# A list product moved behind the last values, and the first pieces of w_out loaded into lasting buffers

## The chip, the core and the metric

The kernel runs on one core of a Trainium2 chip. The metric is the time of one execution on the device, in microseconds (us). Engines are named as in the profile: PE (TensorE, matmuls), DVE (VectorE), ACT (ScalarE), POOL (GpSimd), SP (SyncE, which only issues transfers here).

## The reference

```python
def reference(q, k, v, w_gate, w1, w2, w_in, w_out, s, b):
    # attention: 4 batches, 8 heads, 576 queries, head size 64; keys and values pooled by 8 (72 keys)
    k_p, v_p = (z.reshape(4, 8, 72, 8, 64).mean(axis=3) for z in (k, v))
    x = softmax(q @ k_p.T / 8) @ v_p                      # 2304 tokens of 512 numbers
    # routing: 8 experts, top 1; a token is kept if fewer than 576 before it chose its expert
    e = argmax(x @ w_gate); gate = softmax(x @ w_gate)[e]
    x = gate * (relu(x @ w1[e]) @ w2[e]) if kept else 0   # w1: 512x1024, w2: 1024x512
    # last layers, all tokens
    g = s * relu(x @ w_in) ** 2 + b                       # w_in: 512x2048
    return g @ w_out                                      # w_out: 2048x512
```

## The kernel before

Every product of two full-precision operands is made of three matmuls: each operand is split in a high half (a cast by ACT) and a low half (operand less high half, by DVE or POOL), and high x high, high x low and low x high are added up. Such a group over the four parts of a 512-long sum is twelve matmuls.

**Attention and routing** (to about 150 us). The queries are worked off in tiles of up to 128 tokens, batch after batch (five tiles each, the last one of 64). Values (L273, L275) come out of the PE, DVE scales them (L286 to L294) and leaves them in `xr` and the gate's logits in `lg`. `route(b, t0, t1)` then finds each token's expert (`rmx`, `rd`, `rval`, `rvm`, `roh`: a one-hot row) and its rank in the expert's list by matmuls with a triangle (L368 to L376), called "the ranking" below. Batch 4 is ranked twice, for its first three tiles and for its last two. `tail` makes of the ranks the operands of a list product (`rslot`, `rkey`, `tok`, `ohq`, `rlo`, `ohp`); `tok` holds the token numbers, which GpSimd makes in each tail (L401). `add_lists` is the list product (L434) and adds to `u_lists` (L437). `picked` (L689) reads from the lists the rows of the next unit, and `gather` fetches those with three indirect DMAs on GpSimd's queue (L938). These are Python generators; `step()` advances the queues `todo` (routes) and `tails` in turn, a generator that yields True is blocked for now, `window()` holds one until PE has a place for its matmul, and the list `work` holds the first unit's transposes (`x_part`, L952) and its layer 1 (L961, blocks f of twelve matmuls), which are set between them. The order of instructions on each engine is the order in which this Python code issues them.

**Experts.** `block(u)` works off units of 288 tokens of one expert (150 to 298 us), `small` the short rests of 144. SP loads w1 (L914) and w2 (L920) of the next unit by numbers that DVE makes (`u_i`, L682). Beside this DVE, ACT and POOL turn w_in from 64-bit floats, read as pairs of int32, into 32-bit ones: `Weights64` does a piece of 128x512 in four steps (L868 to L877: shift, or, or, |hi| on ACT, product), with the splitting of the piece before in step 1. `last(s)` is the end of the small experts: layer 2 of the last of them, store of its result yo to yt, and the first blocks of the last layers.

**Last layers.** `pair()` treats the first two units of 256 tokens together: `first(u, ..)` is layer 1 (L1034, twelve matmuls per block f) with `square` (relu by ACT, square by DVE, L1412) and `parts` (gh by ACT, gl by POOL or DVE, L1427); `second(u, ..)` is layer 2 (L1432). Between their blocks `conv(n)` does n steps of the conversion of w_out: 16 pieces `wo`, the splitting of a piece being a cast by ACT (L1386) and a difference by DVE (L1387), and a running sum of the pieces `raw[3]` (L1392). `load_out` loads the pieces on SP's queue (L1458). Layer 2 of the two units begins with the blocks 0 to 6; layer 1 of unit 1 is cut there in two. After the pair come six units, one after the other (`unit`, 442 to 600 us), and an end (`half`).

## Time and profile before

| | us |
|---|---|
| median of 3 runs | 660.01 (657.16 to 661.97) |
| the profiled execution | 664.05 |
| its span from the first to the last instruction | 662.3 |

| stretch of the span (us) | what is in it | PE busy (us) | granted clock (1 is full) |
|---|---|---|---|
| 108 to 152 | end of the attention, layer 1 of the first unit | 31.17 of 44 | 0.88 |
| 152 to 298 | units of the experts | 138.08 of 146 | 0.99 |
| 298 to 325 | small experts | 22.63 of 27 | 0.81 |
| 325 to 364 | end of the small experts, start of the pair | 33.10 of 39 | 0.99 |
| 364 to 409 | pair, to its second half of layer 1 | 38.77 of 45 | 0.50 (first 6 us), 0.98 |
| 409 to 442 | pair, end | 32.44 of 33 | 0.55 (first 6 us), 1.00 |
| 442 to 600 | six units | 158.00 of 158 | 1.00 |

PE is busy for 592.1 us in all (89% of the span), DVE for 365.5, ACT for 253.6 and POOL for 265.8. Busy PE time counts a matmul at the clock that it was given, so time lost to the lower clock is in it.

### The profile page before, as it was taken

To read this page: it belongs to the slowest core of one execution; us is meant where nothing else is said; L and a number is where in the kernel's file an instruction comes from. 1 tells how busy PE (TensorE), PEld (TensorE's weight loads), DVE (VectorE), ACT (ScalarE), POOL (GpSimd) and SP (SyncE) were. 2 spreads that over 40 slices of the span, in tenths; PEclk is the share of its full clock that TensorE was granted. 3 is DMA by queue.
4 is the path that set the end of the run, shared out by engine and by line. 5 is a ranking of instruction groups with operands and counts; after the bars stand their busy time and mean duration, and the time that the engine had idled before them with its cause. 6 is when DMAs were issued, how large, how long until landed. Compare 5 with 4: busy or idle time off the path is not lost. (4 is left out here: it accounts for less than half of the span.)

```text
span 662.3 us, 11174 instructions
## 1 busy us (share of the span) xinstructions
PE 592.1 (89%) x4005; PEld 549.5 (83%) x4005; DVE 365.5 (55%) x889; ACT 253.6 (38%) x620; POOL 265.8 (40%) x384
## 2 busy tenths in 40 slices
PE   5787888769899979997897996999999999999884
PEld 5787777669899979996897976889899899898784
DVE  4688798867968956661639999603312021131140
ACT  1354555436456645442336524304125033042130
POOL 5658434715154716012214301305725145144281
PEclk8799899879999989996999898999999999999998
DMA  8989665645649894844548111017300101000000
GB/s 165 199 183 190 163 195 171 215 126 197 232 155 295 282 309 148 282 135 156 169 142 350 38 33 32 1 33 286 111 17 1 49 17 29 29 9 2 35 2 20
DMA packets 67951, 86.12 MB, mean 130 GB/s; under 512 B 24713, under 2 KB 40073, under 8 KB 67856
## 3 DMA queue, kind: packets, MB, share of 16 engines
q1 hardware_dynamic: 57696, 71.34, 35.9%
q10 hardware_dynamic: 7712, 6.84, 3.4%
q0 software_dynamic: 2448, 6.82, 3.1%
q8 instruction: 42, 0.69, 0.5%
q14 instruction: 53, 0.43, 0.2%
HBM read 68.09 MB, written 17.58 MB: 129 GB/s over the span
## 5 line engine op out<-in xcount | busy, mean ns | idle before, releaser
L1432 PE MATMUL bank<-wo,gh 128*128 128x512 f32 (+1 forms) x412 | 119.3, 374 | 1.2 <-ACT wo L1386 1.0
L1427 POOL TENSOR_TENSOR gl<-rt,gh 128x256 fp32r<-128x256 f32 (+1 forms) x96 | 72.6, 761 | 110.8 <-ACT gh L1426 64.7
L1432 PEld LDWEIGHTS bank<-wo,gh 128*128 128x128 f32 x412 | 74.9, 188 | 15.1 <-ACT wo L1386 1.4
L1432 PE MATMUL bank<-wo,gl 128*128 128x512 f32 (+1 forms) x206 | 76.8, 373 | 0.0
L930 POOL TENSOR_TENSOR w1l<-kraw,w1h 128x128 fp32r<-128x128 f32 x96 | 52.6, 582 | 50.7 <-ACT w1h L923 50.6
L1108 PE MATMUL bank<-hs,w2h 128*128 128x288 f32 (+1 forms) x308 | 68.5, 311 | 4.7 <-issue 4.3
L1439 DVE SCALAR_TENSOR_TENSOR raw<-bank,sb,c_u 128x512 f32<-128x512 f32 (+1 forms) x14 | 9.9, 710 | 85.5 <-PE bank L1432 85.5
L1108 PEld LDWEIGHTS bank<-hs,w2h 128*128 128x128 f32 x308 | 50.7, 192 | 5.6 <-issue 5.1
L1411 ACT ACTIVATE rt<-tq 128x256 f32<-128x256 f32 (+1 forms) x26 | 9.5, 367 | 113.5 <-PE tq L1034 91.3
L1108 PE MATMUL bank<-hs,w2l 128*128 128x288 f32 (+1 forms) x148 | 44.7, 302 | 0.0
L1432 PEld LDWEIGHTS bank<-wo,gl 128*128 128x128 f32 x206 | 38.8, 188 | 6.8
L1412 DVE SCALAR_TENSOR_TENSOR rt<-bank,rt 128x256 f32<-128x256 f32 (+1 forms) x53 | 21.2, 401 | 38.3 <-ACT rt L1411 37.9
L1426 ACT CAST gh<-rt 128x256 fp32r<-128x256 f32 (+1 forms) x96 | 36.6, 381 | 6.5 <-DVE rt L1412 6.5
L938 POOL DMA_INDIRECT xg<-xd,u_idx x23 | 25.4, 1104 | 30.0 <-DVE r L288 16.7
L1440 POOL DMA_INDIRECT out_dram<-raw,it x12 | 12.0, 1001 | 62.6 <-DVE raw L1439 62.1
L1411 ACT ACTIVATE rt<-bank 128x256 f32<-128x256 f32 (+1 forms) x60 | 22.3, 371 | 35.4 <-PE bank L1034 27.0
L228 PE MATMUL sc<-kbd,qT 128*128 128x144 f32 (+1 forms) x152 | 25.4, 316 | 5.6 <-DVE r L286 3.6
L1412 DVE SCALAR_TENSOR_TENSOR rt<-tq,rt 128x256 f32<-128x256 f32 (+1 forms) x24 | 9.6, 400 | 36.3 <-ACT rt L1411 36.3
L1108 PEld LDWEIGHTS bank<-hs,w2l 128*128 128x128 f32 x148 | 28.4, 192 | 0.0
L228 PEld LDWEIGHTS sc<-kbd,qT 128*128 128x128 f32 (+1 forms) x152 | 21.9, 201 | 7.7 <-issue 5.1
L934 DVE TENSOR_TENSOR w2l<-vraw,w2h 128x512 fp32r<-128x512 f32 x39 | 27.4, 702 | 1.2 <-ACT w2h L933 0.5
L961 PE MATMUL bank<-xs,w1h 128*128 128x288 f32 (+1 forms) x120 | 26.1, 303 | 2.1 <-DVE hs L964 2.1
(485 smaller groups left out, 1705.0 us busy)
## 6 DMA issues: line engine op xcount, KB each, us to landing
kraw<-in_moe_w_dram SPq DMA_DIRECT2D x14, 1024.0 KB
vraw<-in_moe_w_dram SPq DMA_DIRECT2D x14, 1024.0 KB
wo<-in_moe_w_out_dram SPq DMA_DIRECT2D x16, 512.0 KB
c_raw<-in_moe_w_in_dram ACTq DMA_DIRECT2D x13, 512.0 KB
kraw<-in_k_dram SPq DMA_DIRECT2D x8, 576.0 KB
out_dram<-c_u SPq DMA_DIRECT2D x1, 4608.0 KB
q<-in_q_dram SPq DMA_DIRECT2D x16, 256.0 KB
xd<-xr SPq DMA_DIRECT2D x16, 256.0 KB
```

The source lines that it names most:

```text
L228: nc.tensor.matmul(sc[:n, p // 2, p % 2 * 144:p % 2 * 144 + 144], lhsT=q[:, p, :n], rhs=kbd[b % 2][:, p], start=True, stop=True)
L930: eng.tensor_sub(self.w1l[:, i, z], self.w1(i)[:, z], self.w1h[:, i, z])
L934: eng.tensor_sub(self.w2l[i], self.w2r[:, i], self.w2h[i])
L938: self.nc.gpsimd.indirect_dma_start(out=dst, out_offset=None, in_=self.xd[:have], in_offset=bass.IndirectOffsetOnAxis(ap=idx[:n], axis=0), ...
L961: self.nc.tensor.matmul(p, lhsT=l[:, f, k], rhs=r[k], start=n == 0, stop=n == 3 * KD - 1)
L1108: nc.tensor.matmul(py[d][:, :v.n], lhsT=l[f][:, d * P:d * P + P], rhs=r[f], start=f == 0 and i == 0, stop=f == KF - 1 and i == 2)
L1411: nc.scalar.activation(r, p, AF.Relu)
L1412: nc.vector.scalar_tensor_tensor(out=p if inside else r, in0=p, scalar=0.0, in1=r, op0=ALU.max, op1=ALU.mult)
L1426: nc.scalar.copy(h[:, :n], r)
L1427: (nc.gpsimd if p is None else nc.vector).tensor_sub(l[:, :n], r, h[:, :n])
L1432: nc.tensor.matmul(p[:, c], lhsT=g[:, j * P:j * P + P], rhs=wo[f][:, z, c], start=f == 0 and i == 0, stop=f == KF2 - 1 and i == 2)
L1440: i = nc.gpsimd.indirect_dma_start(out=dst, out_offset=bass.IndirectOffsetOnAxis(ap=ids, axis=0), in_=o[:, c], in_offset=None, bounds_chec ...
```

## The change

1. The token numbers of all tiles are made once, at the start of the attention, in `toks`; a tail reads its part of it.
2. The tail of batch 3 (`b == B - 2`) waits until one ranking short of the last, so its list product stands behind the last tile's values. With it the pick of unit 1's rows (L689) and their gather move behind the last ranking. Two parts of layer 1 instead of one follow now on the first ranking of batch 4, not on the second.
3. In `last_layers` the first three pieces of w_out use the buffers `c_raw` of w_in's raw pieces, which now live in a pool `keep` that lasts; the buffers `c_f` and `c_u` of the conversion come from the long-lived pools, and gl and the other pieces from a pool `side`. Twelve steps of the conversion (`conv(4 * FIRST)`) stand ahead of the first block. For these three pieces |hi| is made by DVE, the cast of the splitting and the start of the sum by GpSimd; `onesf` is set behind two of those casts.
4. `last` stores yo on ACT's queue, not SP's, splits y at f 6 and 7 and not 4 and 5, and the raw piece 15 of w_in is loaded three steps earlier.

```diff
+        toks = one.tile([P, B, NB], F32, name="toks")
+        nc.gpsimd.iota(toks, pattern=[[S, B], [P, NB]], base=0, channel_multiplier=1, allow_small_or_imprecise_dtypes=True)
...
-            nc.gpsimd.iota(tok, pattern=[[P, w]], base=b * S + t0 * P, channel_multiplier=1, allow_small_or_imprecise_dtypes=True)
...
-            v.scalar_tensor_tensor(out=tok, in0=r, scalar=float(cap), in1=tok, op0=ALU.is_lt, op1=ALU.mult)
+            v.scalar_tensor_tensor(out=tok, in0=r, scalar=float(cap), in1=toks[:, b, t0:t1], op0=ALU.is_lt, op1=ALU.mult)
...
+            while b == B - 2 and now[0] < N - 1:
+                yield True
             yield from window()
             add_lists(b, at_pe[0])
...
-                    for _ in range(2 if ranks == 1 else 1):
+                    for _ in range(2 if ranks == 0 else 1):
                         next(work, None)
...
-                self.nc.scalar.activation(u, t.bitcast(F32)[:, :, 1], AF.Abs)
+                if i < self.alone:
+                    v.tensor_scalar(out=u.bitcast(I32), in0=hi, scalar1=0x7FFFFFFF, scalar2=None, op0=ALU.bitwise_and)
+                else:
+                    self.nc.scalar.activation(u, t.bitcast(F32)[:, :, 1], AF.Abs)
...
-            self.c_raw.append(self.m.tile([P, DM, 2], I32, name=f"c_raw{i - 9}"))
+            self.c_raw.append(self.keep.tile([P, DM, 2], I32, name=f"c_raw{i - 9}"))
...
-                    if pos[0] == 3 or pos[0] % 4 == 2 and pos[0] > 6:
-                        self.load_raw(max(3, pos[0] // 4 + 2), queue)
+                    if pos[0] in (3, MARK - 1) or pos[0] % 4 == 2 and 6 < pos[0] < MARK:
+                        self.load_raw(KF2 - 1 if pos[0] == MARK - 1 else max(3, pos[0] // 4 + 2), queue)
...
+            col = nc.values_load(ti[0:1, 2, self.t.NV + s:self.t.NV + s + 1], engines=[ET.Activation], min_val=0, max_val=T)
...
-                if early and f in (4, 5):
+                if early and f in (6, 7):
...
-            store_small(s)
+            store_y(sid(s), yo(s % 2, SM), SM, nc.scalar, col)
...
-    gl = pool.tile([P, KF2, CU], F32R, name="gl")
-    wo = [pool.tile([P, DM, 2], I32, name=f"wo{i}") for i in reversed(range(KF2))][::-1]
+    gl = side.tile([P, KF2, CU], F32R, name="gl")
+    FIRST = len(x.c_raw)
+    place_out = lambda i, shape, dt: x.keep.tile(shape, dt, name=f"c_raw{i}") if i < FIRST else side.tile(shape, dt, name=f"wo{i}")
+    wo = [place_out(i, [P, DM, 2], I32) for i in reversed(range(KF2))][::-1]
...
     def split_out(i, f):
-        w = wo[i] = pool.tile([P, 2, DM], F32R, name=f"wo{i}")
-        nc.scalar.copy(w[:, 0], f)
+        w = wo[i] = place_out(i, [P, 2, DM], F32R)
+        if i < FIRST:
+            nc.gpsimd.tensor_copy(w[:, 0], f)
+        else:
+            nc.scalar.copy(w[:, 0], f)
...
-            nc.scalar.copy(raw[3], f)
+            nc.gpsimd.tensor_copy(raw[3], f)
...
-        nc.gpsimd.memset(onesf, 1.0)
...
+        conv(4 * FIRST)
+        nc.gpsimd.memset(onesf, 1.0)
         first(0, 0, KF2, ps)
         first(1, 0, HEAD, ph)
```

At the end of the attention PE had this order before, from the last tile but one's values on (`ohp,ohq` is the list product of batch 3, `xg` the transposes of the first unit, `u_lists` the pick, `roh` the first ranking of batch 4, and layer 1 of the first unit follows):

```order
L275 MATMUL o<-vx_163,eT 128x2x73 x2
L434 MATMUL o<-ohp,ohq 48x96 x5
L952 MATMUL tq<-ident,xg_147 128x96 x3
L952 MATMUL misc<-ident,xg_147 128x96 x3
L952 MATMUL te<-ident,xg_147 128x96 x3
L952 MATMUL tq<-ident,xg_147 128x96 x3
L273 MATMUL sc<-vx_163,eT 64x146 x4
L275 MATMUL sc<-vx_163,eT 64x2x73 x2
L689 MATMUL sc<-u_small,u_lists 96x4
L368 LDWEIGHTS tri
L368 MATMUL sc<-roh_1657,tri 128x24
```

And after the change:

```order
L277 MATMUL o<-vx_166,eT 128x2x73 x2
L958 MATMUL tq<-ident,xg_150 128x96 x3
L958 MATMUL misc<-ident,xg_150 128x96 x3
L958 MATMUL te<-ident,xg_150 128x96 x3
L958 MATMUL tq<-ident,xg_150 128x96 x3
L275 MATMUL sc<-vx_166,eT 64x146 x4
L277 MATMUL sc<-vx_166,eT 64x2x73 x2
L437 MATMUL sc<-ohp,ohq 48x96 x5
L370 LDWEIGHTS tri
L370 MATMUL sc<-roh_1630,tri 128x24
```

The list product moved from ahead of the four transposes to behind the last tile's values; the pick is gone from here and stands behind the second ranking.

DVE, between the last tile's values (`lt` and `lg` are its gate's logits) and the one-hot rows `roh` of the second ranking, before:

```order
L290 TENSOR_TENSOR xr_176<-sc,r 64x512
L292 TENSOR_TENSOR lt<-sc,r 64x64
L404 TENSOR_SCALAR rkey_1698<-rslot_1696 128x3
L405 SCALAR_TENSOR_TENSOR tok_1699<-rr_1691,tok_1699 128x3
L294 TENSOR_REDUCE lg_174<-lt 64x8
L408 TENSOR_TENSOR ohq<-rkey_1698,q_179 128x144
L409 TENSOR_SCALAR rlo_1697<-rkey_1698 128x3
L411 TENSOR_TENSOR rlo_1697<-rlo_1697,rslot_1696 128x3
L412 TENSOR_TENSOR ohq<-ohq,tok_1699 128x144
L414 TENSOR_TENSOR ohp<-rlo_1697,p_180 128x288
L324 TENSOR_SCALAR xr_176<-xr_176,rgs_1659 128x512
```

And after, to the one-hot rows' reduction:

```order
L292 TENSOR_TENSOR xr_179<-sc,r 64x512
L294 TENSOR_TENSOR lt<-sc,r 64x64
L296 TENSOR_REDUCE lg_177<-lt 64x8
L326 TENSOR_SCALAR xr_179<-xr_179,rgs_1632 128x512
L340 TENSOR_REDUCE rmx_1695<-lg_177 128x2
L343 TENSOR_TENSOR rd_1697<-lg_177,rmx_1695 128x16
L348 SCALAR_TENSOR_TENSOR rval_191<-rd_1697,rev 128x2x8
L351 TENSOR_REDUCE rvm_1701<-rval_191 128x2
L354 TENSOR_TENSOR roh_1703<-rval_191,rvm_1701 128x16
L356 TENSOR_REDUCE rgs_1705<-rde_189 128x2
```

The tail of the three tiles (`rkey` to `ohp`) left the way between `lt` and `rmx`; it now stands behind the second ranking, with the pick's two operations.

SP ahead of the last layers, before (the last branch of the small experts, then the loads of w_out):

```order
L1021 DMA yr<-yt 128x4x256
L1022 DMA it_1955<-idc 128x2x1
L1113 REGISTER_ALU
L1113 DMA yt<-yo 128x4x144
L1346 UNCONDITIONAL_BRANCH
L1458 DMA wo_16963<-in_moe_w_out_dram 128x1024
L1458 DMA wo_16962<-in_moe_w_out_dram 128x1024
L1458 DMA wo_16961<-in_moe_w_out_dram 128x1024
```

And after:

```order
L952 REGISTER_ALU
L952 DMA idc<-yr 2x96
L1027 DMA yr<-yt 128x4x256
L1028 DMA it_1955<-idc 128x2x1
L1354 UNCONDITIONAL_BRANCH
L1471 DMA c_raw_17083<-in_moe_w_out_dram 128x1024
L1471 DMA c_raw_17082<-in_moe_w_out_dram 128x1024
L1471 DMA c_raw_17081<-in_moe_w_out_dram 128x1024
L1471 DMA wo_17080<-in_moe_w_out_dram 128x1024
```

The store of yo is no longer in SP's queue, and the first three loads write `c_raw`.

DVE at the start of the last layers, before (`rt` squares, L868 to L877 conversion steps):

```order
L877 SCALAR_TENSOR_TENSOR c_f_1975<-c_u_1977,c_f_1975 128x512
L1346 UNCONDITIONAL_BRANCH
L1412 SCALAR_TENSOR_TENSOR rt_1968<-tq,rt_1968 128x256
L868 TENSOR_SCALAR c_f_16943<-wo_16963 128x512
L1412 SCALAR_TENSOR_TENSOR rt_1969<-misc,rt_1969 128x256
L871 SCALAR_TENSOR_TENSOR c_f_16943<-wo_16963,c_f_16943 128x512
L1412 SCALAR_TENSOR_TENSOR bank_1942<-bank_1942,rt_1970 128x256
L873 SCALAR_TENSOR_TENSOR c_f_16943<-wo_16963,c_f_16943 128x512
```

And after, the last of the twelve steps and the first squares:

```order
L871 TENSOR_SCALAR c_f_17063<-c_raw_17081 128x512
L874 TENSOR_SCALAR c_u_17065<-c_raw_17081 128x512
L877 SCALAR_TENSOR_TENSOR c_f_17063<-c_raw_17081,c_f_17063 128x512
L1400 TENSOR_TENSOR c_raw_17124<-c_f_17064,c_raw_17124 128x512
L879 SCALAR_TENSOR_TENSOR c_f_17063<-c_raw_17081,c_f_17063 128x512
L1405 TENSOR_TENSOR raw_1963<-raw_1963,c_f_17064 128x512
L883 SCALAR_TENSOR_TENSOR c_f_17063<-c_u_17065,c_f_17063 128x512
L1425 SCALAR_TENSOR_TENSOR rt_1968<-tq,rt_1968 128x256
L871 TENSOR_SCALAR c_f_17064<-wo_17080 128x512
L1425 SCALAR_TENSOR_TENSOR rt_1969<-misc,rt_1969 128x256
L877 SCALAR_TENSOR_TENSOR c_f_17064<-wo_17080,c_f_17064 128x512
```

All steps of the first three pieces now stand ahead of the first square; the next piece's follow between the squares.

## Rows read from the trace of the kernel before

**Rows 1.** Chain that ended last: start, us, engine, tile, line, instructions.
```profile
414.82 2.83 PE bank L1034 x24
417.64 24.59 PE bank L1432 x108
```

**Rows 2.** PE timeline, last layers: start, us, instruction, [idle before <- releaser].
```profile
346.27 0.40 PE L1034 MATMUL tq<-yhl,w2h 128*128 128x256 f32 x2
...
363.85 0.58 PE L1034 MATMUL tq<-y1l,w1h 128*128 128x256 f32 x1 [2.63 <-DVE y1l L1027]
...
384.83 0.50 PE L1432 MATMUL bank<-wo,gh 128*128 128x512 f32 x1 [1.00 <-ACT wo L1386]
...
406.10 0.39 PE L1034 MATMUL bank<-y1h,w2h 128*128 128x256 f32 x1 [3.79 <-DVE rt L1412]
...
409.56 0.58 PE L1034 MATMUL tq<-y1h,w2h 128*128 128x256 f32 x1 [1.77 <-DVE gl L1427]
```

**Rows 3.** Windows: length, busy PE, PEld, DVE, ACT, POOL, granted clock, DMA share, GB/s.
```profile
409.00:415.00 6.00, 5.44 (x27) 5.45 (x28) 3.93 (x9) 1.17 (x5) 1.98 (x2) 0.55 0.00 0
```

**Rows 4.** SP timeline: DMA issues.
```profile
145.70 1.50 SPq L914 DMA_DIRECT2D kraw<-in_moe_w_dram  x2
...
328.09 1.04 SPq L1022 DMA_DIRECT2D it<-idc  x1
...
335.47 0.39 SPq L1113 DMA_DIRECT2D yt<-yo  x1
...
339.62 0.35 SPq L1458 DMA_DIRECT2D wo<-in_moe_w_out_dram  x1
```

**Rows 5.** DVE timeline, last layers.
```profile
332.60 1.43 DVE L1027 TENSOR_TENSOR yhl<-yr,yhl 128x256 fp32r<-128x256 f32 x4 [7.66 <-ACT yhl L1026]
...
344.11 0.43 DVE L868 TENSOR_SCALAR c_f<-wo 128x512 int32<-128x512 int32 x1 [6.63 <-DMA wo<-in_moe_w_out_dram]
...
398.64 0.42 DVE L868 TENSOR_SCALAR c_f<-wo 128x512 int32<-128x512 int32 x1
...
400.03 0.69 DVE L1387 TENSOR_TENSOR wo<-c_f,wo 128x512 fp32r<-128x512 f32 x1 [0.24 <-ACT wo L1386]
...
402.44 0.42 DVE L868 TENSOR_SCALAR c_f<-wo 128x512 int32<-128x512 int32 x1
```

**Rows 6.** PE timeline, end of the attention.
```profile
128.73 0.51 PE L961 MATMUL tq<-xs,w1h 128*128 128x288 f32 x2
...
130.41 0.43 PE L961 MATMUL misc<-xs,w1h 128*128 128x288 f32 x2
...
137.52 0.20 PE L368 MATMUL o<-roh,tri 128*128 128x16 bf16 x1 [5.37 <-DVE roh L352]
...
137.71 0.83 PE L961 MATMUL te<-xs,w1h 128*128 128x288 f32 x2
...
149.04 1.15 PE L434 MATMUL o<-ohp,ohq 128*48 128x96 f32 x10
...
150.62 0.50 PE L1108 MATMUL bank<-hs,w2h 128*128 128x288 f32 x2 [0.43 <-DVE u_lists L437]
```

**Rows 7.** DVE timeline, end of the attention.
```profile
134.75 0.16 DVE L405 SCALAR_TENSOR_TENSOR tok<-rr,tok 128x3 f32<-128x3 f32 x1 [4.11 <-POOL tok L401]
...
142.91 0.35 DVE L414 TENSOR_TENSOR ohp<-rlo,p 128x192 f32<-128x192 f32 x1
```

**Rows 8.** POOL (GpSimd) timeline, end of the attention and small experts.
```profile
134.57 0.24 POOL L401 IOTA tok<- 128x3 f32 x2
...
317.51 1.47 POOL L1084 TENSOR_TENSOR w1l<-c_f,w1h 128x512 fp32r<-128x512 f32 x1 [11.11 <-ACT w1h L1083]
...
318.94 1.73 POOL L1046 TENSOR_TENSOR w2l<-raw,w2h 128x512 fp32r<-128x512 f32 x1
```

**Rows 9.** DVE timeline, small experts, beside the last two of rows 8.
```profile
317.99 1.55 DVE L1046 TENSOR_TENSOR w2l<-raw,w2h 128x512 fp32r<-128x512 f32 x1
...
319.46 1.76 DVE L873 SCALAR_TENSOR_TENSOR c_f<-c_raw,c_f 128x512 int32<-128x512 int32 x1
```

More of the change, by code (lines that the diff above doesn't have):

```diff
@@ L852, with __init__ @@
 class Weights64:
-    def __init__(self, nc, pieces, raw, out, f, u, late=None):
-        self.nc, self.raw, self.out, self.f, self.u, self.late = nc, raw, out, f, u, late
+    def __init__(self, nc, pieces, raw, out, f, u, late=None, alone=0):
+        self.nc, self.raw, self.out, self.f, self.u, self.late, self.alone = nc, raw, out, f, u, late, alone
         self.pieces, self.total = pieces, 4 * pieces + (3 if late else 2)
@@ L887, in __init__ @@
             self.n, self.xh, self.xl, self.hh, self.hl = n, x[:KD], x[KD:2 * KD], h[:KF], h[KF:2 * KF]
-    def __init__(self, nc, tc, c, a, left, m, xd, idc, yt, hist, cap, capp):
+    def __init__(self, nc, tc, c, a, left, keep, m, xd, idc, yt, hist, cap, capp):
         self.__dict__.update({k: v for k, v in locals().items() if k != "self"})
@@ L1076, in main @@
         queue = nc.scalar
-        c_f = [one.tile([P, DM], I32, name=f"c_f{i}") for i in range(2)]
+        c_f = [left.tile([P, DM], I32, name=f"c_f{i}") for i in range(2)]
         def out(i, f):
@@ L1086, in main @@
         cv = Weights64(nc, KF2, lambda i: self.c_raw[i % 3], out, lambda i: self.raw[i].bitcast(I32) if i < KF else c_f[i % 2],
-                       [one.tile([P, DM], F32, name=f"c_u{i}") for i in range(2)])
+                       [(left, one)[i].tile([P, DM], F32, name=f"c_u{i}") for i in range(2)])
         NU, cap, capp = self.t.NU, self.cap, self.capp
@@ L1108, in layer2, with store_y @@
                     nc.tensor.matmul(py[d][:, :v.n], lhsT=l[f][:, d * P:d * P + P], rhs=r[f], start=f == 0 and i == 0, stop=f == KF - 1 and i == 2)
-        def store_y(u, y, n):
+        def store_y(u, y, n, queue=nc.sync, col=None):
             for d in range(KD):
                 nc.scalar.copy(y[:, d], py[d][:, :n])
-            nc.sync.dma_start(out=self.yt.rearrange("(d p) n -> p d n", p=P)[:, :, cols(u, n)], in_=y)
+            queue.dma_start(out=self.yt.rearrange("(d p) n -> p d n", p=P)[:, :, bass.ds(regs[u][1] if col is None else col, n)], in_=y)
         def store_unit(u, v=self.v):
@@ L1359, in main, with last_layers @@
         rest_small(1)
-def last_layers(nc, tc, c, a, pool, x, ps, out):
+def last_layers(nc, tc, c, a, pool, side, x, ps, out):
     NV = -(-T // CU)
@@ L1372, in last_layers @@
     x.yp.append(y)
-    cf, cu = [pool.tile([P, DM], I32, name=f"c_f{i}") for i in range(2)], [pool.tile([P, DM], F32, name="c_u0")]
+    cf, cu = [x.w.tile([P, DM], I32, name=f"c_f{i}") for i in range(2)], [x.w.tile([P, DM], F32, name="c_u0")]
     gh = pool.tile([P, KF2, CU], F32R, name="gh")
-    gl = pool.tile([P, KF2, CU], F32R, name="gl")
-    wo = [pool.tile([P, DM, 2], I32, name=f"wo{i}") for i in reversed(range(KF2))][::-1]
+    gl = side.tile([P, KF2, CU], F32R, name="gl")
+    FIRST = len(x.c_raw)
+    place_out = lambda i, shape, dt: x.keep.tile(shape, dt, name=f"c_raw{i}") if i < FIRST else side.tile(shape, dt, name=f"wo{i}")
+    wo = [place_out(i, [P, DM, 2], I32) for i in reversed(range(KF2))][::-1]
     ph, po = ps[0:4], ps[4:8]
@@ L1467, in pair @@
                     nc.sync.dma_start(out=sb[:, j:j + 1], in_=a[n].unsqueeze(0).to_broadcast([P, 1]))
-        more.extend(pool.tile([P, 2, 2, CU], F32R, name=f"wo{i}") for i in range(KF2 - 2, KF2))
+        more.extend(side.tile([P, 2, 2, CU], F32R, name=f"wo{i}") for i in range(KF2 - 2, KF2))
         spare.extend(x.w.tile([P, 2, CU], F32R, name=f"raw{i}") for i in range(3))
         held = []
-        nc.gpsimd.memset(onesf, 1.0)
         def first(u, f0, f1, banks):
@@ L1500, in pair @@
         for i in range(KF2 - 2, KF2):
-            wo[i] = pool.tile([P, DM, 2], I32, name=f"wo{i}")
+            wo[i] = place_out(i, [P, DM, 2], I32)
             load_out(i)
@@ L1509, in pair @@
         raw[0:3] = [x.w.tile([P, DM], F32, name=f"raw{i}") for i in range(3)]
-        slots.extend(raw[2:4] + [pool.tile([P, DM], F32, name="c_f1")])
-        sums["drop"] = pool.tile([P, DM], F32, name="c_u0")
+        slots.extend(raw[2:4] + [x.w.tile([P, DM], F32, name="c_f1")])
+        sums["drop"] = x.w.tile([P, DM], F32, name="c_u0")
     def unit(u):
@@ L1609, in program @@
                     x.main(w, m1, ps)
+            side = es.enter_context(tc.tile_pool(name="s", bufs=1, side="right"))
             pool = es.enter_context(tc.tile_pool(name="n", bufs=1))
-            last_layers(nc, tc, c, a, pool, x, ps, out)
+            last_layers(nc, tc, c, a, pool, side, x, ps, out)
 def kernel(**inputs):
```

10 lines of the change are left out of this document (6 added, 4 removed).

## The prediction

> **What bounds the kernel now.** I read the chain that ended last first: its last long stretches are matmuls, L1432 for 24.59 us from 417.64 and the 24 matmuls ahead of it [rows 1]. TensorE (PE) sets the end, so an edit is worth what it takes out of PE's waits and out of the time that PE spends at the lower clock. Then I looked for those waits in PE's timeline, at the two places that the change touches.
>
> Place one is `pair()` of the last layers. PE waits 2.63 us at 363.85 for the low halves of y1, 1.00 at 384.83 for a converted piece of w_out, 3.79 at 406.10 for a squared tile and 1.77 at 409.56 for gl [rows 2]. All four releases stand in VectorE's (DVE's) queue among the conversion steps, or behind them, so DVE is the bound there. After the last of them the granted clock of the stretch is 0.55 [rows 3], which is the lower level (1.2 GHz) for nearly all of it: the 24 matmuls from 409.56 to 414.82 take 5.26 us, the next 24, of the same shape, 2.83 [rows 1, 2]. That is 2.43 us more. Why is DVE late? SP issues the y store at 335.47 and the first w_out piece only at 339.62 [rows 4]. That piece releases DVE at 344.11, 4.49 us after its issue, while DVE had finished its last split at 332.60 + 1.43 = 334.03 [rows 5]: ten idle microseconds ahead of a stretch that it bounds.
>
> Place two is the end of the attention. PE waits 5.37 us at 137.52 for the one-hot rows of the second ranking of batch 4 [rows 6]. DVE had waited 4.11 us at 134.75 for the token numbers `tok` [rows 7], which GpSimd makes at 134.57, behind the gathers in its queue [rows 8]. After PE's wait a pair of L961 matmuls takes 0.83 us where it took 0.43 at 130.41. One block f took 1.68 us (128.73 to 130.41), six of them would take 10.08, and from 137.71 to 149.04 they took 11.33 [rows 6]: 1.25 us lost to the lower clock.
>
> **The change, part by part.** *Token numbers made once, list product and pick of batch 3 moved.* The wait of 4.11 us goes, since nothing between the gathers and DVE's product is left. DVE alone would then let the second ranking start at 137.52 - 4.11 = 133.4, and a little earlier as the three-tile tail (`rslot` to `ohp`) moves behind it. PE finishes the second block f at about 130.41 + 1.68 = 132.1 and has the moved list product (0.5 to 1 us) in front of it: 132.7 to 133.4. I take 133.0, so 4.5 us are gained, and with the 1.25 us of clock 5.75. What is late next? DVE now does both tails and the pick's additions behind the second ranking. The last `ohp` ended at 143.26, 5.74 after the ranking [rows 6, 7]. Behind a ranking at 133.0, with the three-tile tail (at most 2.8 us, since 134.75 to 137.52 holds it) and with one w2l product and two more hs products set ahead of it (some 2 us), it ends at 143 to 143.5; PE's layer 1 would end at 149.04 - 5.75 = 143.3. So the list product waits little, 0 to 1 us. The other thing that can be late is w1 of unit 1: SP issues it at 145.70 [rows 4], released by numbers that the same DVE queue makes after the second ranking, and these come only 1 to 2 us earlier, while layer 2 starts (150.62 before) 5 us earlier. How much spare time that load has, no row shows: nothing lost if it has 4 us, all but 1 or 2 us lost if it has none. I take 1.6 us for these two together. The gather of unit 1 moves behind the second ranking; it is needed only for work behind 150.62, and costs nothing. **Attention: 4.1 us gained**, bounds 1 and 5.75.
>
> *First three pieces of w_out in lasting buffers, y store on ScalarE's (ACT's) queue.* The three loads no longer wait for the memory of yo, and SP no longer stands before the store. SP's last transfer ahead of them is done issuing at 328.09 + 1.04 = 329.13 [rows 4]; with 4.49 us to landing the first piece is there at 333.6, and DVE is free at 334.03. The store costs ACT one issue, and ACT is idle there until PE's first tile, so that costs nothing; without that cover, some 0.4 us.
>
> *Twelve conversion steps ahead of the first squares.* A piece took 3.80 us (398.64 to 402.44), of which 0.24 was a wait for ACT's cast [rows 5]. The twelve steps are three pieces, 11.4 us, less one low half and two sums that fall behind them (3 x 0.69), less the waits (3 x 0.24), with three |hi| more (at 0.42, as a one-input operation of this size takes): 9.9 us. They end at 334.0 + 9.9 = 343.9, were DVE alone. It is not: three of the four casts and copies that move to GpSimd run beside them. Where GpSimd ran 128x512 operations (317.51, 318.94) [rows 8], DVE's two-input operations of that size took 1.55 and 1.76 us [rows 9] and not 0.69: 0.86 to 1.07 more each. Three of the five operations of a piece have two inputs, so I take 3/5 of 0.97 for each of three: 1.7 us. The steps end at 345.6. PE comes back to its first bank at 346.27 [rows 2], and the first square is done by then or just behind: nothing lost.
>
> *What follows from it.* From 344.11 to 363.80 DVE did fourteen steps, the squares and the halves of y1 without a pause, 19.7 us. After the change it does the next fourteen steps from 345.6 on, with one low half and two sums more (2.1 us): the halves of y1 are ready at 367.4 and PE waits 3.6 us longer at that place. From there DVE has twelve steps (11.4 us) less to do, which is more than the waits left: 1.00 + 3.79 + 1.77 = 6.56 [rows 2], and 2.43 of clock with them: 9.0 us. Next bound behind that is PE itself. **Last layers: 9.0 - 3.6 = 5.4 us gained.** With no price for GpSimd it is 7.1, with whole GpSimd operations (below) 2.7, with loads landing 2 us later 3.4.
>
> *The rest* (the split of y at f 6 and 7, the load of piece 15 three steps earlier, which now stands ahead of the copies of yo in one path, the memory pools) lies beside PE work with time to spare, or moves nothing; if the load holds ACT up, 1 us.
>
> Sum: 4.1 + 5.4 = 9.5 us. The profiled execution took 664.05 (span 662.3); it would take 654.5. It lies 4.0 above the median of the runs, 660.0, so the forecast for the median is **650.5**.
>
> **The Trainium skill** speaks against the casts on GpSimd. In "SBUF — State Buffer", section "Who interferes with whom", it says that a DVE instruction with two SBUF inputs contends with a GpSimd instruction that reads SBUF, and that whoever issues first makes the other wait for the whole instruction. The trace agrees: DVE's operation of 319.46 ended at 321.22, 0.55 us after GpSimd's of 318.94 (320.67) [rows 8, 9]. By that section the sum is that of rival A, 653.2; by the share of operations taken above it is 650.5.
>
> **The rivals.** *A, GpSimd blocks DVE whole.* If each of the three operations costs DVE its full 1.47 us (317.51) [rows 8], the steps end at 348.3, PE waits 2 us at its ninth block, and the last layers gain 2.7: 653.2. For it: the two rows both show DVE ending half a microsecond behind GpSimd. Against it: the steps have one-input operations in which a cast can hide.
>
> *B, the attention gives its gain back.* If DVE's two tails and the load of w1 take the place of the waits removed, 1 us is left there: 653.6. For it: the load's numbers come out of the same queue. Against it: PE's layer 2 of unit 0 (from 150.62) lies ahead of unit 1's weights, with its own steps.
>
> *C, slower: the loads come no earlier.* SP's loads may still stand behind a wait at the end of the branch, for the y store or for the last reader of the buffers. Then the twelve steps begin at 344.1 as before, but all squares stand behind them: the halves of y1 come 10 us later than in the forecast, and the last layers lose 5. It decides from a landing of about 339.4, where the gain of 5.4 is used up. PE would then wait some 10 us at its ninth block (346.27) and lose again the 2.4 us of a slow restart: 660.0 - 4.1 + 5 + 2.4 = 663. Against it: the new buffers are not those of yo, and their last reader is DVE's work ahead of 332.60.
>
> *D, better.* If GpSimd's operations hide wholly and nothing is late in the attention, both places reach their bounds: 660.0 - 5.75 - 7.1 = 647.2.
>
> **How the numbers follow.** Forecast 0.48, A 0.15, B 0.17, C 0.10, D 0.10. A measurement of this kernel can tell about 1% (6.6 us) from no change; faster begins below 653.4. That holds for most of the forecast (0.42), D, and a little under half of A and B (0.14): 0.66. Same takes the rest of A and B and most of C: 0.27. Slower is C with a larger stall: 0.07. The range reaches from D, with the runs' own scatter of some 2.4 below it, to short of C: 643.5 to 657.5.
>
> **What the profile would show.** Right: no DVE wait for `tok`; PE's second ranking near 133 and the L961 matmuls behind it at the upper clock; the first w_out load on SP near 329 and DVE's first step near 334; a PE wait for y1 of 5 to 7 us near 367, and none of over 0.5 us from there to the L1432 stretch that ended at 442. Wrong: a first landing behind 339, a wait of PE at its ninth block of the last layers, or layer 2 of unit 0 starting near 150.

## The result and the profile after

The changed kernel takes 650.94 us (median of 4 runs, 647.89 to 655.13) where the kernel before took 658.59 beside it (4 runs): a ratio of 0.989, 95% interval 0.9855 to 0.9926, which is 4.9 to 9.5 us less. The forecast was 650.5 us, 9.5 less. The gain is clear of zero; whether it exceeds the 1% that the prediction drew as its line, the interval leaves open.

The profiled execution after took 649.79 us, with a span of 648.1, 14.2 less than the profiled one before. That pair flatters the change. To see which part of it is the change, I cut the span at five instructions: the first layer-2 matmul of unit 0, the first `bank<-rt,vraw` matmul of the small experts, the first `tq<-yhl,w1h` of the pair of last layers, and the start of the long stretch of 108 matmuls. In us, from PE's timeline of each profiled execution; the first line is the start of unit 0's layer 2, the others are differences. The other columns are the kernels of the experiments, by whether that stretch is as before or as after in them:

| stretch | before | after | others, stretch as before | others, stretch as after |
|---|---|---|---|---|
| to layer 2 of unit 0 | 150.62 | 144.43 | 148.41 | 142.91 to 146.66 (10 profiles) |
| to the small experts' first layer 2 | 152.06 | 151.65 | 153.29 to 153.60 (3) | 150.44 to 151.84 (9) |
| to the pair | 32.19 | 28.10 | 29.03, 29.13 | 27.79 to 31.22 (10) |
| pair, to the long stretch | 82.77 | 77.98 | 80.22, 80.93 | 78.05 to 78.95 (3) |
| from there to the end | 244.66 | 245.94 | 243.79, 244.69 | 245.04 to 246.02 (6) |

The third line swings by 3 to 4 us between profiles in both columns, so its 4.1 us in this pair say nothing of the change (the means differ by 0.9). By the means of all profiles as before and as after, the other lines give 149.5 - 144.6 = 4.9, 153.1 - 151.3 = 1.8 and 81.3 - 78.3 = 3.0 us gained and 245.7 - 244.4 = 1.3 lost: 8.4 us, inside the interval of the runs.

**Attention.** The PE timeline of the changed kernel (start, us, instruction, idle before it and what ended it), which answers to [rows 6]:

```profile
123.15 0.47 PE L958 MATMUL tq<-ident,xg 96*128 96x96 f32 x3 [3.75 <-DVE xs L960]
...
131.64 0.18 PE L370 MATMUL o<-roh,tri 128*128 128x16 bf16 x1
...
133.63 0.43 PE L967 MATMUL te<-xs,w1h 128*128 128x288 f32 x2
...
142.84 1.15 PE L437 MATMUL o<-ohp,ohq 128*48 128x96 f32 x10
...
144.43 0.51 PE L1113 MATMUL bank<-hs,w2h 128*128 128x288 f32 x2 [0.43 <-DVE u_lists L440]
```

The second ranking at 131.64 has no wait (5.37 before), the pairs of layer 1 behind it take 0.43 and not 0.83, and the last list product follows without a wait. The DVE timeline, for [rows 7]: the token numbers and the last one-hot rows.

```profile
137.96 0.15 DVE L406 SCALAR_TENSOR_TENSOR tok<-rr,toks 128x3 f32<-128x3 f32 x1
...
142.52 0.34 DVE L415 TENSOR_TENSOR ohp<-rlo,p 128x192 f32<-128x192 f32 x1
```

No idle time stands at `tok`, and `ohp` ends at 142.86, when PE comes to its product. SP issues w1 of unit 1 at 143.12 (145.70 before):

```profile
143.12 1.05 SPq L920 DMA_DIRECT2D kraw<-in_moe_w_dram  x2
```

**Last layers.** SP's and ACT's transfers [rows 4]: the first three pieces of w_out are issued at 319.10, and the store stands on ACT, behind them in time.

```profile
317.76 0.67 SPq L1028 DMA_DIRECT2D it<-idc  x1
319.10 1.30 SPq L1471 DMA_DIRECT2D c_raw<-in_moe_w_out_dram  x3
...
324.81 0.43 ACTq L1118 DMA_DIRECT2D yt<-yo  x1
```

DVE [rows 5]: its idle time between its last split and the first conversion step is 1.60 us. Before, it was 9.7 in two pieces, 3.03 ahead of a first square at 337.06 and the 6.63 ahead of the step at 344.11. The twelve steps run from 324.62 to 335.49.

```profile
321.59 1.43 DVE L1033 TENSOR_TENSOR yhl<-yr,yhl 128x256 fp32r<-128x256 f32 x4 [7.05 <-ACT yhl L1032]
324.62 0.43 DVE L871 TENSOR_SCALAR c_f<-c_raw 128x512 int32<-128x512 int32 x1 [1.60 <-DMA c_raw<-in_moe_w_out_dram]
324.96 0.42 DVE L874 TENSOR_SCALAR c_u<-c_raw 128x512 int32<-128x512 int32 x1
325.30 0.68 DVE L877 SCALAR_TENSOR_TENSOR c_f<-c_raw,c_f 128x512 int32<-128x512 int32 x1
...
327.69 0.83 DVE L874 TENSOR_SCALAR c_u<-c_raw 128x512 int32<-128x512 int32 x1
328.44 1.09 DVE L877 SCALAR_TENSOR_TENSOR c_f<-c_raw,c_f 128x512 int32<-128x512 int32 x1
...
331.72 0.84 DVE L874 TENSOR_SCALAR c_u<-c_raw 128x512 int32<-128x512 int32 x1
...
335.49 0.41 DVE L1425 SCALAR_TENSOR_TENSOR rt<-tq,rt 128x256 f32<-128x256 f32 x1
...
339.00 0.42 DVE L1425 SCALAR_TENSOR_TENSOR bank<-bank,rt 128x256 f32<-128x256 f32 x1
...
341.47 0.41 DVE L1440 TENSOR_TENSOR gl<-bank,gh 128x256 fp32r<-128x256 f32 x1
```

GpSimd's casts beside them, which the forecast had priced from [rows 8]:

```profile
327.56 0.68 POOL L1397 CAST c_raw<-c_f 128x512 fp32r<-128x512 f32 x1 [11.05 <-DVE c_f L883]
328.20 0.80 POOL L1407 COPY raw<-c_f 128x512 f32<-128x512 f32 x1
331.53 0.75 POOL L1397 CAST c_raw<-c_f 128x512 fp32r<-128x512 f32 x1 [2.54 <-DVE c_f L883]
```

PE in the pair, which answers to [rows 2]. The waits of 1.00, 3.79 and 1.77 us are gone but for 0.41. In front of the y1 wait a new one of 2.90 stands at the eleventh block, and one of 0.62 at the ninth.

```profile
335.95 0.50 PE L1040 MATMUL tq<-yhl,w2h 128*128 128x256 f32 x2 [0.62 <-DVE rt L1425]
...
341.94 0.50 PE L1040 MATMUL bank<-yhl,w2h 128*128 128x256 f32 x2 [2.90 <-DVE gl L1440]
...
358.24 0.58 PE L1040 MATMUL tq<-y1l,w1h 128*128 128x256 f32 x1 [2.63 <-DVE y1l L1033]
...
394.93 0.39 PE L1040 MATMUL bank<-y1h,w2h 128*128 128x256 f32 x1 [0.41 <-DVE rt L1425]
```

Windows (length, busy PE, PEld, DVE, ACT, POOL, granted clock, DMA share, GB/s): the clock falls behind each of the two large waits, and is whole where it was 0.55 before [rows 3].

```profile
342.00:348.00 6.00, 6.00 (x38) 6.00 (x39) 6.00 (x13) 3.73 (x11) 3.06 (x4) 0.72 1.02 410
358.00:364.00 6.00, 5.76 (x30) 5.77 (x31) 5.33 (x12) 3.15 (x8) 1.05 (x2) 0.57 0.35 92
396.00:402.00 6.00, 6.00 (x55) 5.94 (x53) 2.81 (x8) 3.17 (x10) 2.70 (x5) 1.00 0.00 1
```

And the chain that ended last, for [rows 1]:

```profile
399.44 2.72 PE bank L1040 x24
402.16 24.99 PE bank L1445 x108
...
450.69 22.20 PE bank L1445 x96
```

The 24 matmuls ahead of the stretch take 2.72 us, the upper clock. But the 108 matmuls take 24.99 us where they took 24.59, at a whole clock and with no wait in them: something that no step of the prediction had.

**Small experts.** The load of piece 15, three steps earlier, holds ACT for 4 us at a time when PE has other work, and PE's first layer-2 matmul there then waits 2.24 us. In the profiles with the load at its old place it waits 4.2 to 4.3.

```profile
283.25 4.13 ACTq L976 DMA_DIRECT2D c_raw<-in_moe_w_in_dram  x2
287.42 1.52 ACT L1117 COPY yo<-bank 128x352 f32<-128x352 f32 x4 [3.61 <-DMA c_raw<-in_moe_w_in_dram]
```

```profile
296.08 1.22 PE L1248 MATMUL bank<-rt,vraw 128*128 128x144 f32 x8 [2.24 <-ACT w1h L1089]
```

### The profile page after: what moved, and what is told of

It reads as the page before. It is cut to its first block, busy times and chain, and to the rows that moved or that the text cites. A ratio compares the mean times of both kernels' runs of the same rounds, so it can differ in the third digit from the quotient of the medians.

```text
span 648.1 us, 11186 instructions
## 1 busy us (share of the span) xinstructions
PE 588.7 (91%) x4005; PEld 545.1 (84%) x4005; DVE 367.0 (57%) x893; ACT 249.9 (39%) x614; POOL 267.8 (41%) x384
## 5 line engine op out<-in xcount | busy, mean ns | idle before, releaser
L1440 POOL TENSOR_TENSOR gl<-rt,gh 128x256 fp32r<-128x256 f32 (+1 forms) x96 | 71.3, 747 | 99.3 <-ACT gh L1439 57.9
L1445 PE MATMUL bank<-wo,gh 128*128 128x512 f32 (+1 forms) x340 | 99.2, 376 | 0.0
L1445 PEld LDWEIGHTS bank<-wo,gh 128*128 128x128 f32 x340 | 62.0, 188 | 12.2
L1445 PE MATMUL bank<-wo,gl 128*128 128x512 f32 (+1 forms) x170 | 63.8, 375 | 0.0
L1445 PEld LDWEIGHTS bank<-wo,gl 128*128 128x128 f32 x170 | 31.9, 188 | 6.5
L230 PEld LDWEIGHTS sc<-kbd,qT 128*128 128x128 f32 (+1 forms) x152 | 21.9, 201 | 8.4 <-issue 4.9
```

What stands on the lines that cost most here:

```text
L230: nc.tensor.matmul(sc[:n, p // 2, p % 2 * 144:p % 2 * 144 + 144], lhsT=q[:, p, :n], rhs=kbd[b % 2][:, p], start=True, stop=True)
L1440: (nc.gpsimd if p is None else nc.vector).tensor_sub(l[:, :n], r, h[:, :n])
L1445: nc.tensor.matmul(p[:, c], lhsT=g[:, j * P:j * P + P], rhs=wo[f][:, z, c], start=f == 0 and i == 0, stop=f == KF2 - 1 and i == 2)
```

## The experiments

All these kernels compute the whole output. Ratios are to the kernel before, in the same set of runs; the interval is 95%. Kernels of one set share the runs of before: e1 to e4 (658.62 us); e6, e7 and both e9 (659.08); e8, e10 and e11 (660.38); e12 (658.65).

**e1: the attention's part alone**, on the kernel before: the first four hunks of the change (`toks`, its use, the `while`, `ranks == 0`).

> Only the attention's part of the change (token numbers made once, list product and pick moved, two parts of layer 1 on the first ranking). Theory (the two parts add up): PE's 5.37 us wait ahead of the second ranking is gone, layer 1 behind it runs at the upper clock, layer 2 of the first unit starts 4.5 to 5.5 us earlier, and the last layers keep all their waits (2.63, 1.00, 3.79, 1.77 us): 4.5 to 5.5 us below before, ratio 0.992 to 0.993. Rival (what is gained in the attention is given back among the experts, whose weights come no earlier): layer 2 starts earlier, but the small experts start less than 2 us earlier, ratio 0.997 to 1.0.

Measured: 654.20 us, 0.9937 (0.9904 to 0.9971), 4.1 us less; layer 2 of unit 0 starts at 144.66. The attention's term is of the forecast size.

**e2: the last layers' part alone**: the change without those four hunks.

> Only the part in the last layers (lasting buffers, store of yo on ACT, twelve steps ahead). Theory: from PE's first L1034 matmul to its long L1432 stretch some 78 us as in the changed kernel and not 82.8, attention as before: 4 to 5 us below before, ratio 0.992 to 0.994. Rival (the last layers gain only because the small experts ahead of them happened to run at the upper clock in the one profile): no more than 1.5 us, ratio 0.998 to 1.0.

Measured: 656.13 us, 0.996 (0.9931 to 0.999), 2.6 us less. The pair takes 78.05 us, and the stretch behind it 245.97. 4.1 and 2.6 come near the 7.2 us of the whole (0.989 of 658.6): the parts add, and the last layers give half of their term; the 5.4 us forecast for them lie outside e2's interval (0.7 to 4.5 us).

**e3: the token numbers alone**, with the list product and the pick where they were.

```diff
+        toks = one.tile([P, B, NB], F32, name="toks")
+        nc.gpsimd.iota(toks, pattern=[[S, B], [P, NB]], base=0, channel_multiplier=1, allow_small_or_imprecise_dtypes=True)
...
-            nc.gpsimd.iota(tok, pattern=[[P, w]], base=b * S + t0 * P, channel_multiplier=1, allow_small_or_imprecise_dtypes=True)
...
-            v.scalar_tensor_tensor(out=tok, in0=r, scalar=float(cap), in1=tok, op0=ALU.is_lt, op1=ALU.mult)
+            v.scalar_tensor_tensor(out=tok, in0=r, scalar=float(cap), in1=toks[:, b, t0:t1], op0=ALU.is_lt, op1=ALU.mult)
```

> Only the token numbers made once; list product, pick and gather stay where they were. Theory (the wait for the token numbers is the whole cost in the attention): DVE's wait of 4.11 us goes, the second ranking comes 3.5 to 4.1 us earlier, layer 2 of the first unit 3.5 to 5 us earlier, ratio 0.993 to 0.995. Rival (the list product's place ahead of the last values matters as much): PE keeps a wait of 2 us or more ahead of the second ranking and layer 2 starts no more than 2.5 us earlier, ratio 0.996 to 1.0.

Measured: 654.37 us, 0.9928 (0.9903 to 0.9954). PE's timeline keeps a wait of 1.23 us at the second ranking:

```profile
134.51 0.18 PE L370 MATMUL o<-roh,tri 128*128 128x16 bf16 x1 [1.23 <-DVE roh L354]
...
145.96 0.50 PE L1109 MATMUL bank<-hs,w2h 128*128 128x288 f32 x2 [0.43 <-DVE u_lists L438]
```

It is as fast as e1. The token numbers are the whole gain that can be measured. What the moved list product takes off here, e1 and the changed kernel wait earlier: 3.75 us in one piece for the first unit's transposed tokens (123.15 above), 2.44 in e3.

**e4: the store of the small expert back on SP**, the rest of the change kept.

```diff
-            store_y(sid(s), yo(s % 2, SM), SM, nc.scalar, col)
+            store_small(s)
```

> The changed kernel with the store of yo back on SP's queue, so that the first three loads of w_out stand behind it again while the twelve steps still stand ahead of the squares. Theory of the prediction's rival C: the first load lands 5 to 6 us later, PE waits 6 us or more at its ninth block of the last layers and restarts at the lower clock, the halves of y1 come as much later, and the last layers lose all of their 4.8 us and 1 to 5 us more: 656 to 662, ratio 0.997 to 1.006. Against it (the early load is not what matters, the twelve steps' place is): within 2 us of the changed kernel, ratio 0.988 to 0.992.

Measured: 656.93 us, 0.9977 (0.9943 to 1.0011). The first loads on SP, then DVE and PE:

```profile
325.46 1.31 SPq L1471 DMA_DIRECT2D c_raw<-in_moe_w_out_dram  x3
```

```profile
330.26 0.43 DVE L871 TENSOR_SCALAR c_f<-c_raw 128x512 int32<-128x512 int32 x1 [7.77 <-DMA c_raw<-in_moe_w_out_dram]
```

```profile
341.59 0.80 PE L1040 MATMUL tq<-yhl,w2h 128*128 128x256 f32 x2 [6.63 <-DVE rt L1425]
```

The loads come some 6 us later (319.10 after), and the pair takes 84.57 us, 6.6 more than in the changed kernel and more than with the old part. This is rival C's mechanism: steps put ahead of the squares make a late load dearer than it was. The early loads need the store off SP's queue.

**e6: |hi| of the first three pieces on ACT again.**

```diff
-... lambda i, f, b=b: add(b + i, f), 0 if b else FIRST)
+... lambda i, f, b=b: add(b + i, f), 0)
```

> The changed kernel with |hi| of the first three pieces back on ACT; casts stay on GpSimd. Theory (DVE's twelve steps are the delay, each operation taken from them counts): the steps end some 1.8 us earlier (three operations of 0.34 to 0.75 us start to start), the last low half of y1 and PE's second part of the pair come 1.5 to 2 us earlier, ratio 0.986 to 0.987. Rival (ACT's relus then stand behind its |hi| and DVE's squares wait for them, or DVE's gain is taken up by GpSimd's operations): within 0.7 us of the changed kernel, 0.988 to 0.990.

Measured: 651.38 us, 0.988 (0.9836 to 0.9925). The twelve steps take 10.1 us and not 10.9; the pair takes 77.89 us. That fits the rival: DVE's three operations more cost nothing that can be measured.

**e7: the halves of y1 split at blocks 6 to 9 and not 10 to 13.**

```diff
-                if u == 0 and 10 <= f < 10 + KD:
-                    x.split_y(1, f - 10, nc.vector)
+                if u == 0 and 6 <= f < 6 + KD:
+                    x.split_y(1, f - 6, nc.vector)
```

> The changed kernel with the splits of y1 set behind the blocks 6 to 9 of the first unit and not 10 to 13. DVE's work stays the same in sum. Theory (PE's wait of 2.63 us and the slow restart behind it come from the place of y1's low halves in DVE's queue): no PE wait over 0.5 us for y1, the stretch behind it at the upper clock, 2 to 4 us below the changed kernel, ratio 0.983 to 0.986. Rival (DVE is the bound and only the place of the wait moves): PE waits 2 us or more for squares before or behind that place, or for a converted piece, and the pair takes as long as in the changed kernel, within 0.7 us, ratio 0.988 to 0.990.

Measured: 648.45 us, 0.9855 (0.9815 to 0.9895); the pair 77.27 us. The y1 wait is gone, and PE's timeline has another of 3.12 us:

```profile
361.47 0.39 PE L1040 MATMUL tq<-y1h,w1h 128*128 128x256 f32 x1 [3.12 <-DVE rt L1425]
```

A step set earlier in DVE's queue sets a square later. The two readings differ: the ratio is the theory's, 2.3 us below the changed kernel, but the intervals overlap; the pair of the profile is only 0.7 us shorter, as the rival has it. By the profile the amount of DVE's work decides here, and its order only where PE waits; the runs leave it open.

**e8: the loads early, but no steps ahead of the first unit.**

```diff
-        conv(4 * FIRST)
```

> The changed kernel without the twelve steps ahead of the first square (the call is left out; all steps stand between the blocks, as before the change); loads as early as in the changed kernel, so DVE waits for no load. Theory (DVE's whole work in the pair is the bound, and the early loads are what lets it begin; where the steps stand matters little): no PE wait ahead of the ninth block, the waits come later instead, the pair (first L1034 matmul to the long L1432 stretch) takes 77 to 80 us as against 78.0 in the changed kernel and 80.2 to 82.8 before, ratio 0.987 to 0.992. Rival 1 (the steps ahead are the gain, as the prediction has it): 80.5 us or more, ratio 0.993 or more. Rival 2 (the steps ahead only hold up the squares): 75 us or less, ratio below 0.986.

Measured: 651.58 us, 0.9871 (0.9845 to 0.9897), as fast as the changed kernel. Its profiled execution has a pair of 83.40 us, 5.4 longer. But at 656.33 us it was the slowest of its eight, so it doesn't stand for the median (its layer 2 of unit 0 alone starts 2 us later than the mean of the others); e12 takes this up.

**e9: the start addresses of the streamed tiles.** In the built program the change's new pools put `wo`, `c_raw` and `gl` at odd multiples of 32 bytes of a partition; before, `wo` and `gl` stood at multiples of 128. An unused tile of 96 bytes shifts them. In e9_align_all it stands behind the last `c_raw`, and every tile of L1445 starts at a multiple of 128; in e9_align_most it stands ahead of the first, and the three `c_raw` stay at multiples of 32 alone.

```diff
             self.load_raw(i - 9, nc.sync)
+            if i == 11:
+                self.keep.tile([P, 24], F32, name="pad")
```

> The changed kernel with a tile of 96 bytes per partition added behind the three lasting buffers, which moves c_raw, gl and the other pieces of w_out from start addresses that are multiples of 32 bytes to multiples of 128, as they were before the change; nothing else differs. Theory (the 96 matmuls L1432 of a unit take 22.20 us instead of 21.80 because of where their operands start): 21.80 us again in every unit, the time from the start of the long stretch to the end 244 to 244.7 us instead of 246, 1.3 to 2 us below the changed kernel, ratio 0.986 to 0.987. Rival (something else in the new pools or the moved memory makes them slower): 22.20 us stay, ratio 0.989.

> The same tile of 96 bytes ahead of the three lasting buffers: gl and pieces 3 to 15 start at multiples of 128 bytes, the three c_raw buffers still at multiples of 32. If it is the streamed operand's start that counts, the three-matmul groups that read c_raw stay at 0.693 us and those that read wo go to 0.68: a unit takes 21.85 to 21.9 us. If it is the start of gl, which every group loads as weights, all groups go to 0.68 and a unit takes 21.80. If neither, 22.20.

Measured: e9_align_all 647.99 us, 0.9836 (0.9797 to 0.9875); e9_align_most 650.03 in a single run. The chains, of e9_align_all and then of e9_align_most:

```profile
403.02 24.59 PE bank L1447 x108
451.26 21.80 PE bank L1447 x96
```

```profile
402.53 24.59 PE bank L1447 x108
450.76 21.99 PE bank L1447 x96
```

In e9_align_all the 0.40 us in each stretch are gone with the address. The same holds in e9_align_most for the stretch of 108, which streams no `c_raw`. In its stretch of 96, which the expectation had at 21.85 to 21.9, a group of three matmuls that streams a `c_raw` takes 0.70 to 0.71 us and one that streams a `wo` mostly 0.68 (from start to start in PE's timeline; `gh` and `gl`, which are loaded as weights, are the same in both):

```profile
451.30 0.64 PE L1447 MATMUL bank<-c_raw,gh 128*128 128x512 f32 x2
...
452.01 0.63 PE L1447 MATMUL bank<-c_raw,gh 128*128 128x512 f32 x2
...
454.79 0.62 PE L1447 MATMUL bank<-wo,gh 128*128 128x512 f32 x2
...
455.47 0.62 PE L1447 MATMUL bank<-wo,gh 128*128 128x512 f32 x2
```

So the start of the streamed operand costs, at the same clock. In the changed kernel, where `gl` too starts at an odd multiple of 32, all groups take 0.69 to 0.70; why the `c_raw` groups are a little dearer with `gl` aligned stays open.

After the pair come four whole units and not six, so there are five long stretches. The chain leaves out the last, which takes 22.20 us too (before: 599.03 to 620.82, 21.79):

```profile
584.18 0.63 PE L1445 MATMUL bank<-c_raw,gh 128*128 128x512 f32 x2
...
606.38 1.05 PE L1565 MATMUL tq<-yr,raw 128*128 128x128 f32 x8
```

**e10: the load of piece 15 at its old place**, the rest of the change kept.

```diff
-                    if pos[0] in (3, MARK - 1) or pos[0] % 4 == 2 and 6 < pos[0] < MARK:
-                        self.load_raw(KF2 - 1 if pos[0] == MARK - 1 else max(3, pos[0] // 4 + 2), queue)
+                    if pos[0] == 3 or pos[0] % 4 == 2 and pos[0] > 6:
+                        self.load_raw(max(3, pos[0] // 4 + 2), queue)
```

> The changed kernel with the load of w_in's piece 15 at its old place, three steps later. Theory (that place, which the prediction took for nothing, is what shortens PE's wait at the first small expert from 4.3 to 2.0 us): the wait is 4 us or more again and the stretch from the first unit's layer 2 to there 152.5 to 153.5 us instead of 151.2, 1.5 to 2.2 us slower than the changed kernel, ratio 0.991 to 0.993. Rival (the lasting buffers or chance did it): wait near 2 us, ratio 0.989.

Measured: 661.82 us, 1.0026 (1.0006 to 1.0046): with this one condition undone the whole gain is gone, some 9 us (from 0.989). SP's first load of w_out is issued 10.3 us behind the transfer ahead of it (320.37), after the change 1.3. Below stand that load and, from the list of SP's waits between 315 and 340 (us in total, times, longest), what it waited for:

```profile
330.69 2.40 SPq L1471 DMA_DIRECT2D c_raw<-in_moe_w_out_dram  x3
```

```profile
SPq L1471 <- DMA yt<-yo: 9.1, 1, 9.1
```

PE, at the small experts and at the ninth block of the pair:

```profile
296.27 2.26 PE L1248 MATMUL bank<-rt,vraw 128*128 128x144 f32 x8 [4.17 <-issue]
...
346.06 0.80 PE L1040 MATMUL tq<-yhl,w2h 128*128 128x256 f32 x2 [7.66 <-DVE rt L1425]
```

The first load of w_out goes into the buffer of piece 15, and must wait for that piece's load. In the built program it carries a wait on one DMA semaphore more than in the changed kernel, and by the trace what ended it was the landing of the small expert's store, which ACT issued at 327.47. The built program says why: the load of piece 15, in the branch without small experts, and the store, in the branch that ran here, count on that same semaphore, and the wait behind the branches asks for the value that only the store's landing completes here. No run changes this alone. The pair takes 86.36 us, 8.4 more than after: rival C once more, by another way.

**e11: aligned, y1 at blocks 6 to 9, no steps behind blocks 0 to 5 of the first unit**, to take the new waits away together.

```diff
+        if i == 11:
+            self.keep.tile([P, 24], F32, name="pad")
...
-                conv(1, steps_of_first)
-                if u == 0 and 10 <= f < 10 + KD:
-                    x.split_y(1, f - 10, nc.vector)
+                if u or f >= 6:
+                    conv(1, steps_of_first)
+                if u == 0 and 6 <= f < 6 + KD:
+                    x.split_y(1, f - 6, nc.vector)
```

> The changed kernel with three edits: the tile of 96 bytes that sets the starts to multiples of 128, the splits of y1 at blocks 6 to 9, and no conversion step behind the blocks 0 to 5 of the first unit (the steps move into places later that were left empty). Theory (DVE's work is the bound; from the first step to 394.9 it idles only 3 to 4 us, so no more than that is to be had): no wait of 2.9 us at the eleventh block, the pair takes 74.5 to 76.5 us, units 21.80 us, ratio 0.979 to 0.983. Rival (the waits move on to the converted pieces or to y1): pair 77 us or more, ratio 0.984 to 0.986.

Measured: 648.86 us, 0.9826 (0.9798 to 0.9854). The wait at the eleventh block is gone, but PE waits 2.38 us at 360.69 for a square, and 3.73 at the end of the pair, where it waited 3.79 before the change:

```profile
396.13 0.58 PE L1042 MATMUL bank<-y1h,w2h 128*128 128x256 f32 x1 [3.73 <-DVE rt L1427]
```

The pair takes 77.95 us, as the rival has it (77 or more). The ratio is in the theory's range, but nothing sets it apart from e9_align_all (0.9836), so what it has over the changed kernel can all be the alignment's.

**e12: e9_align_all without the steps ahead**, for what e8 left open.

> The kernel of e9_align_all (every tile of the last layers at a multiple of 128 bytes) without the twelve conversion steps ahead of the first unit. Open from e8_no_steps_ahead: its profiled execution, the slowest of its eight, lost 5.4 us in the pair of last layers against the changed kernel, its median nothing. If the steps ahead are worth the 5.4 us of that profile: a ratio near 0.984 + 0.008 = 0.992, and a pair near 83 us in the profile. If their work only moves to where VectorE is just as full, and the store of the small expert holds the first unit back until the same time anyway: a ratio within 0.980 to 0.988, as e9_align_all had (0.9836), and a pair of 77 to 80 us in the profile. In both, 21.80 us for each unit of 96 matmuls and 24.59 for 108, as the addresses are unchanged.

Measured: 651.38 us, 0.988 (0.9845 to 0.9915); the pair 82.93 us, 4.0 more than in e9_align_all. PE's waits at the end of the pair are those of [rows 2] again:

```profile
395.43 0.38 PE L1042 MATMUL bank<-y1h,w2h 128*128 128x256 f32 x1 [3.77 <-DVE rt L1427]
...
398.89 0.58 PE L1042 MATMUL tq<-y1h,w2h 128*128 128x256 f32 x1 [1.65 <-DVE gl L1442]
```

In both profiles without the steps ahead the pair is as long as before the change, although the loads come early. So in the profiles the steps are what turns the early loads into time. How much of that is in the medians stays open: by e12 some 2.9 us against e9_align_all, with overlapping intervals, by e8 none against the changed kernel.

## Why the prediction was right

**Attention, 4.1 forecast.** 4.1 us by e1's ratio, 4.9 by the profiles; rival B fell. The mechanism is the one named: the wait for `tok` and the lower clock behind it. One step of it was idle: the moved list product and pick, which the forecast counted into the ranking's start at 133.0, change nothing that the runs can tell from e3 (0.9937 against 0.9928; in the profiles layer 2 starts 1.3 us earlier with them). Unit 1's load of w1 came only 2.6 us earlier, as feared, but ACT then waited 0.82 us for it and PE none.

**The loads and the twelve steps.** Forecast: the first piece ready and DVE free at about 334.0, steps of 9.9 us and 1.7 for GpSimd. Measured: 5.5 us from issue to DVE's start (4.49 forecast), 10.87 us for the steps (11.6). GpSimd's part, 1.7 us, was 1.25, and mis-sized in each factor. The casts took 0.68 to 0.80 us and not the 1.47 of [rows 8]. Each of the three, not three in five, met a DVE operation and lengthened it, by 0.41, 0.41 and 0.42 us. Two of these (L874) have one input and one (L877) has two, so the argument against rival A, that a cast can hide in one-input operations, fails.

Rival A's sum is not what came (1.25 us against 4.4), but its mechanism held. Each cast had begun 0.13 to 0.24 us before the DVE operation, 0.55 to 0.56 us of it were left, and DVE ended 0.28, 0.53 and 0.28 us after the cast. Alone these operations take 0.42, 0.68 and 0.42, so all but the first 0.14 or 0.15 us of them came after the cast. The two cases of [rows 8, 9] agree: DVE ended 0.56 and 0.55 us after GpSimd, with 0.68 or 0.69 alone. The Trainium skill, "SBUF — State Buffer", section "Who interferes with whom", has DVE wait for the whole GpSimd instruction if that was issued first. The trace agrees with that, but what it makes DVE pay is what is left of the cast. That is 1.67 us for the three, an estimate from the rows, and not three times its whole length.

**What follows from it, 3.6 lost and 9.0 gained.** From the pair's start to y1's last wait PE took 34.06 us after and 28.98 before, 5.1 more; from there to the long stretch 43.92 and 53.79, 9.9 less. So the second term was right, with its clock. The first was too small, and its place was wrong: the wait for y1 did not grow (the same 2.63 us, where 5 to 7 were expected), and PE lost 2.90 us at the eleventh block instead. That block reuses a bank that DVE squares in place at 339.00 and reads for `gl` at 341.47, both behind the twelve steps and some of the next; the forecast held only the ninth block against the end of the steps, and there PE waited 0.62 us (6.63 and 7.66 with the late loads of e4 and e10). The two terms make 4.8 us in this pair of profiles and 3.0 by the means: the profile before has the longest pair of its column (82.77 against 80.22 and 80.93).

**Two terms that were set to nothing.** Of the load of piece 15 and the memory pools the prediction said that they lie *"beside PE work with time to spare"* or move nothing. For the pools that was wrong: the new addresses cost 0.40 us in each of five long stretches, 2.0 in all and 1.3 by the means of the table (e9). For the load it was wrong twice. The load held ACT up for 3.6 us and PE lost nothing by it; instead the small experts begin 1.8 us earlier (the second line of the table). And the early loads exist only with it (e10): it is a condition of the main term, worth some 9 us.

Together the last layers gave 3.0 + 1.8 - 1.3 = 3.5 us by the profiles and 2.6 by e2's ratio (0.7 to 4.5), where 5.4 were forecast. By e2 this is about what rival A gave the last layers (2.7), but not for A's reason, since GpSimd cost less than forecast. The whole was forecast 2 us too high. That 650.94 stands so near to 650.5 is in part luck: the kernel before took 658.59 us beside it and not 660.0, and the two terms set to nothing had opposite signs.

## What to carry to other kernels

Before a load is called free of its old wait, follow every wait that it carries in the new program, those of the earlier user of its buffer too: here two edits of one line each (the store's queue, an older load's place) decide whether the three loads come 6 to 9 us earlier. Work that is put ahead of a consumer's steps pays, by the profiles, if its data are there, and costs more than it gave if they are late (6.6 and 8.4 us in the pair); so the two belong in one experiment. Where a pool is moved, compare the start addresses of the tiles that TensorE streams, and the duration of a stretch of equal matmuls before and after.
